# Deltanet attention and a top-2 router: expert sums kept in the output instead of rows gathered at the end

## The chip, the cores and the metric

The kernel runs on one core of a Trainium2 chip. The metric is the device time of one execution in microseconds. The inputs lie in device memory before it starts, and the output does after it.

## The reference

A gated delta-rule attention gives one row of 384 numbers for each of 3072 tokens; a noisy top-2 router then sends each token through two of eight experts, and the two results are added with weights.

```python
# attention: q, k, v are (4, 8, 768, 48), beta is (4, 8, 768)
k_n = k / (norm(k) + 1e-06)
for t in range(768):
    y[:, :, t] = einsum('bhd,bhde->bhe', q[:, :, t], state)
    v_old = einsum('bhde,bhd->bhe', state, k_n[:, :, t])
    state = state + beta_t * einsum('bhd,bhe->bhde', k_n[:, :, t], v[:, :, t] - v_old)
x = y.transpose(0, 2, 1, 3).reshape(3072, 384)
# router and experts: w1 is (8, 384, 1024), w2 is (8, 1024, 384)
noisy_logits = x @ w_gate + log1p(exp(x @ w_noise)) * noise
top2 = argpartition(-noisy_logits, 2)[:, :2]
top2_w = softmax over the two, with 1e-09 in the denominator
for e in range(8):
    for k in range(2):
        mask = top2[:, k] == e
        out[mask] += top2_w[mask, k, None] * (maximum(x[mask] @ w1[e], 0) @ w2[e])
```

## The kernel before

**Attention.** The 768 positions are cut into 12 chunks of 64, and two chunks are a step. A unit is one chunk of a pair of batches: 128 rows, 384 numbers each; a step has four units. `products(n)` transposes k of a unit (kp to kT) and makes its Gram matrices. `invert(s)` inverts the triangular matrices of a whole step on DVE by 30 pairs of operations that wait for each other (`part` and `t`, L340 and L344); its results are two transposes, `tt` (L355) and `tb` (L356). `join(n)` copies `tt` into `w64` on ACT (L369) and completes it with two products on TensorE (`p_x`), which go through ACT (`x`, L380, and `w64`, L389). `within(n)` transposes q (qp to qT, L269) and multiplies it with kT (`p_q`, then `qk` on DVE, L401). `recur(c)` is the serial part: `v` less what the state predicts (`p_b`, L472), `u`, then the new state `st`. `answer(n)` makes the output rows `y` (L427), and from them the router's logits. The loop over chunks takes a share of each of these at each point; a scheduler of the language then sets the order of every engine's instructions by its own estimates, so that a change in one place can move instructions in another.

**Router.** `route(s)` runs for each step: the two largest noisy logits, the weights, and for each token and choice a slot, which is the row of the expert's list that the token gets. `spread` then writes the token's rows to these slots of `rows_x` in device memory: eight scatters of 128 rows per step, issued by POOL. `rows_x` is cleared first, early in the program (eight SP DMAs), so that unused slots hold zeros.

**Experts.** Each expert has seven tiles of 128 rows, 896 in all. Its rows come in one DMA (`xr`), TensorE transposes them (`p_xt`, copied to `xe` by DVE), `first` multiplies with w1 and applies the relu on ACT (`hT`), and `second` multiplies with w2 (`p_o`) and has DVE copy the result out of PSUM to `yr` (L734), which SP writes to `rows_y`. The weights alternate between two pools; the second one is in memory that attention uses, so its first load waits until attention is over. All loads are issued by SP, in its order. Rows beyond 896 are handled in a branch (L768) that is taken only when some expert has more.

**The end.** For each of 24 tiles of 128 tokens POOL gathers the two expert rows of each token from `rows_y` (L795), ACT multiplies one by its weight (L802), DVE multiplies the other and adds (L803), and SP writes two pieces of the output (L810).

Of the kernel before, what the change touches and what calls it, by code (L numbers as in the profile page):

```python
# [15 lines left out]
C = 64  # L16
DP = 64
Q = 32
TILES = 7
HALF = TILES * 128 // 2  # L20


@with_exitstack
def kernel(
# [12 lines left out]
):  # L37

# [79 lines left out]
    rows_x = tc.dram_tile([E * N, DM], FP32, name="rows_x")  # L118
# [6 lines left out]
    slots = [const.tile([128, NT], I32, name=f"slot{i}") for i in range(2)]  # L125
    gates = [const.tile([128, NT], FP32, name=f"gate{i}") for i in range(2)]
# [35 lines left out]
    written, cleared = [], []  # L162

    def clear(buf, first, last):

        return nc.sync.dma_start(
            out=buf[first:last].rearrange("(t p) d -> p t d", p=128),
            in_=zero[:, None, :].to_broadcast([128, (last - first) // 128, DM]),
        ).ins
# [14 lines left out]
    def deltanet(ictx):  # L184
# [221 lines left out]
        def answer(n):  # L406
# [106 lines left out]
        def route(s):  # L513
# [20 lines left out]
            u, w, d, noisy = (full(x) for x in ("u", "w", "d", "noisy"))  # L534
            nc.scalar.activation(u, ln, ACTF.Abs)
# [19 lines left out]
            def take_largest(x, name):  # L555

                top, at, hit = (
                    per_token(f"{name}_top"), per_token(f"{name}_at"), full(f"{name}_hit")
                )
# [7 lines left out]
            top0, hit0 = take_largest(noisy, "a")  # L567
# [5 lines left out]
            top1, hit1 = take_largest(rest, "b")  # L573
            p1, den = gates[1][:, to], gates[0][:, to]
# [24 lines left out]
            for hit, slot in ((hit0, slots[0]), (hit1, slots[1])):  # L599
# [3 lines left out]
                nc.vector.tensor_copy(slot[:, to], row)  # L603
            for n in range(s * US, (s + 1) * US):
                for slot in slots:
                    yield
                    spread(ys[n], slot[:, n : n + 1])
# [4 lines left out]
            vv(p1, p1, den, ALU.mult)  # L612
# [21 lines left out]
        for e in range(E):  # L634
            cleared.append(clear(rows_x, e * N, e * N + TILES * 128))
        first_weights = load_weights(w_even, 0)

# [124 lines left out]
    most_i = moe.tile([128, 1], I32, name="most_i", bufs=1)  # L762
    p_n = ps([128, E], "p_n")
    nc.tensor.matmul(p_n, ones, before)
    nc.vector.tensor_reduce(out=most, in_=p_n, axis=AX.X, op=ALU.max)
    nc.vector.tensor_copy(most_i, most)
    count = nc.values_load(most_i[0:1, 0:1], min_val=0, max_val=N)
    with tc.If(count > TILES * 128):  # L768
        more = NT - TILES
        w1f = moe_w1.rearrange("e d f -> (e d) f")  # L770
        w2f = moe_w2.rearrange("e f d -> (e f) d")
        for e in range(E):
            with tc.tile_pool(name=f"left{e}", bufs=1) as pool:
# [3 lines left out]
                nc.sync.dma_start(out=w2e, in_=w2r[e])  # L777
                for i in range(TILES, NT):
                    r0 = e * N + i * 128
                    xr = pool.tile([128, 1, DM], FP32, name="xrl")  # L780
                    nc.sync.dma_start(out=xr[:, 0], in_=rows_x[r0 : r0 + 128])
                    xe = pool.tile([128, KT, 128], FP32, name="xel")
# [3 lines left out]
                    yr = pool.tile([128, DM], FP32, name="yrl")  # L786
                    second(w2e, hT, 0, yr)
                    nc.sync.dma_start(out=rows_y[r0 : r0 + 128], in_=yr)


    for n in range(NT):
        got = []
        for slot in slots:
            g = moe.tile([128, DM], FP32, name=f"got{len(got)}", bufs=4)
            nc.gpsimd.indirect_dma_start(  # L795
                out=g,
                out_offset=None,
                in_=rows_y,
                in_offset=bass.IndirectOffsetOnAxis(ap=slot[:, n : n + 1], axis=0),
            )  # L800
            got.append(g)
        nc.scalar.mul(got[0], got[0], gates[0][:, n : n + 1])  # L802
        nc.vector.scalar_tensor_tensor(  # L803
            out=got[0], in0=got[1], scalar=gates[1][:, n : n + 1], in1=got[0],
            op0=ALU.mult, op1=ALU.add,
        )
        c, u = divmod(n, NU)
        for i in range(2):
            t0 = (2 * u + i) * S + c * C
            nc.sync.dma_start(out=out[t0 : t0 + C, :], in_=got[0][i * C : i * C + C])  # L810
# [31 lines left out]
```

## Time and profile before

| | |
|---|---|
| time, median of 3 runs | 1200.49 us (1191.12 to 1205.19) |
| the profiled execution | 1196.75 us, its span 1195.0 us |
| mean granted TensorE clock | 0.813 |
| TensorE (PE) busy | 926.0 us, 77% |
| VectorE (DVE) busy | 325.7 us, 27% |
| ScalarE (ACT) busy | 272.5 us, 23% |
| GpSimd (POOL) busy | 170.7 us, 14% |
| moved by DMA | 124.30 MB, mean 104 GB/s |

The span is the time from the first to the last instruction that the profiler shows; the execution's own time is 1.75 us longer. The busy times are sums over the whole program, which has three stages with different limits: attention and router up to about 484 us, the experts from 511 to 1114 us, and the gathers at the end.

### The profile page before, as it was taken

To read this page: it belongs to the slowest core of one execution; us is meant where nothing else is said; L and a number is where in the kernel's file an instruction comes from. 1 tells how busy PE (TensorE), PEld (TensorE's weight loads), DVE (VectorE), ACT (ScalarE), POOL (GpSimd) and SP (SyncE) were. 2 spreads that over 40 slices of the span, in tenths; PEclk is the share of its full clock that TensorE was granted. 3 is DMA by queue.
4 is the path that set the end of the run, shared out by engine and by line. 5 is a ranking of instruction groups with operands and counts; after the bars stand their busy time and mean duration, and the time that the engine had idled before them with its cause. 6 is when DMAs were issued, how large, how long until landed. Compare 5 with 4: busy or idle time off the path is not lost. (4 is left out here: it accounts for less than half of the span.)

```text
span 1195.0 us, 20175 instructions
## 1 busy us (share of the span) xinstructions
PE 926.0 (77%) x8670; PEld 624.2 (52%) x8670; DVE 325.7 (27%) x875; ACT 272.5 (23%) x645; POOL 170.7 (14%) x222
## 2 busy tenths in 40 slices
PE   3265678788676788089999999999999999999200
PEld 2154667677565676055555555555555555555100
DVE  3867933736456130110200102001020010200122
ACT  3365254354241421011020110201102011020022
POOL 4211123141323111200000000000000000000365
PEclk9657566757666665589999999999999999999655
DMA  5981155234535701431302313023130220000366
GB/s 107 277 266 32 32 179 166 50 98 145 179 128 172 260 12 43 172 124 66 116 17 86 113 66 109 23 86 112 66 102 31 86 66 14 33 0 33 106 197 188
DMA packets 142657, 124.30 MB, mean 104 GB/s; under 512 B 84704, under 2 KB 134880, under 8 KB 142560
## 3 DMA queue, kind: packets, MB, share of 16 engines
q1 hardware_dynamic: 135520, 103.95, 27.9%
q0 software_dynamic: 6144, 18.88, 5.1%
q8 instruction: 70, 1.15, 0.4%
q14 instruction: 27, 0.22, 0.1%
q10 hardware_dynamic: 896, 0.10, 0.1%
HBM read 59.99 MB, written 62.91 MB: 103 GB/s over the span
## 5 line engine op out<-in xcount | busy, mean ns | idle before, releaser
L721 PE MATMUL p_h<-xe,w1e 128*128 128x448 f32 x768 | 291.0, 540 | 1.5 <-DVE xe L715 1.5
L730 PE MATMUL p_o<-w2e,hT 128*128 128x384 f32 x896 | 290.3, 486 | 0.0
L730 PEld LDWEIGHTS p_o<-w2e,hT 128*128 128x128 f32 x896 | 170.2, 190 | 119.6 <-issue 3.0
L721 PEld LDWEIGHTS p_h<-xe,w1e 128*128 128x128 f32 x768 | 145.5, 190 | 143.1 <-issue 139.9
L725 ACT ACTIVATE hT<-p_h 128x448 f32<-128x448 f32 x128 | 69.7, 544 | 527.8 <-PE p_h L721 527.8
L734 DVE COPY yr<-p_o 128x384 f32<-128x384 f32 x56 | 31.2, 557 | 543.4 <-PE p_o L730 543.4
L795 POOL DMA_INDIRECT got<-rows_y,slot x48 | 47.0, 979 | 644.4 <-SPq L768 625.5
L340 DVE TENSOR_TENSOR part<-t 128x30 f32<-128x30 f32 (+9 forms) x180 | 61.5, 342 | 4.8
L172 POOL DMA_INDIRECT rows_x<-y,slot x48 | 49.7, 1036 | 88.5 <-issue 41.8
L344 DVE TENSOR_TENSOR t<-t,part 128x30 f32<-128x30 f32 (+9 forms) x180 | 60.6, 337 | 4.7
L480 PE MATMUL p_u<-v,w 64*64 64x48 f32 x768 | 42.3, 281 | 9.3 <-ACT y L427 8.1
L510 POOL COPY wide<-st 64x384 f32<-64x384 f32 x44 | 23.5, 535 | 161.8 <-DVE st L507 145.7
L480 PEld LDWEIGHTS p_u<-v,w 64*64 64x64 f32 x768 | 40.0, 200 | 12.6 <-issue 9.7
L369 ACT COPY w<-tt 32x256 f32<-32x256 f32 x96 | 38.6, 402 | 31.2 <-DVE tt L355 29.8
L422 PE MATMUL p_y<-u,qk 64*64 64x48 f32 x768 | 45.0, 295 | 0.8 <-issue 0.8
L422 PEld LDWEIGHTS p_y<-u,qk 64*64 64x64 f32 x768 | 41.0, 209 | 5.2 <-issue 5.0
L714 PE MATMUL p_xt<-ident,xr 128*128 128x128 f32 x168 | 21.9, 291 | 27.9 <-DMA xr<-rows_x 27.9
L375 PE MATMUL p_x<-tb,at 32*32 32x32 f32 x768 | 23.4, 229 | 24.4 <-DVE tb L356 22.6
L277 PE MATMUL p_b<-st,kT 64*64 64x48 f32 x704 | 25.8, 269 | 18.9 <-DVE qk L401 15.1
L277 PE MATMUL p_k<-kT 64*64 64x64 f32 x768 | 21.4, 266 | 21.5 <-ACT kT L269 21.5
L802 ACT ACTIVATE got<-got,gate 128x384 f32<-128x384 f32 x24 | 14.7, 614 | 96.9 <-DMA got<-rows_y,slot 91.0
L277 PE MATMUL p_q<-qT,kT 64*64 64x64 f32 x768 | 17.6, 248 | 24.6 <-ACT qT L269 23.7
(121 smaller groups left out, 811.4 us busy)
## 6 DMA issues: line engine op xcount, KB each, us to landing
rows_y<-zero SPq DMA_DIRECT2D x8, 3264.0 KB
w1e<-in_moe_w_dram SPq DMA_DIRECT2D x8, 1536.0 KB
w2e<-in_moe_w_dram SPq DMA_DIRECT2D x8, 1536.0 KB
rows_x<-zero SPq DMA_DIRECT2D x8, 1344.0 KB
xr<-rows_x SPq DMA_DIRECT2D x8, 1344.0 KB
rows_y<-yr SPq DMA_DIRECT2D x56, 192.0 KB
kp<-in_k_dram SPq DMA_DIRECT2D x48, 96.0 KB
qp<-in_q_dram SPq DMA_DIRECT2D x48, 96.0 KB
```

The costliest lines, as they stand in the source:

```text
L172: d = nc.gpsimd.indirect_dma_start(out=rows_x, out_offset=bass.IndirectOffsetOnAxis(ap=slot, axis=0), in_=rows, in_offset=None,).ins
L277: nc.tensor.matmul(out[rows_of[b], z, j], lhsT[rows_of[z], j, rows_of[b]], rhs(rows_of[z], j, b), start=(j == 0), stop=(j == NP - 1), skip ...
L340: nc.vector.tensor_tensor(out=part, in0=t[:, j + 1 :, j, None].to_broadcast(shape), in1=t[:, None, j, 0:j].to_broadcast(shape), op=ALU.mult,)
L344: nc.vector.tensor_tensor(out=t[:, j + 1 :, 0:j], in0=t[:, j + 1 :, 0:j], in1=part, op=ALU.add)
L369: nc.scalar.copy(w64[rows, :, cols], tt[rows])
L422: nc.tensor.matmul(p_y[b, h], qk[b, h % 2, h // 2], u[b, h], start=(c == 0 and h == 0), stop=(h == H - 1), skip_group_check=True,)
L480: nc.tensor.matmul(p_u[b, h], w64[b, h], r[b, h], start=(h == 0), stop=(h == H - 1), skip_group_check=True,)
L721: nc.tensor.matmul(p_h, w1e[:, do, fo * 128 : (fo + 1) * 128], xe[:, do, cols], start=(do == 0), stop=(do == KT - 1),)
L725: nc.scalar.activation(hT[:, fo, cols], p_h, ACTF.Relu)
L730: nc.tensor.matmul(p_o, hT[:, fo, i * 128 : (i + 1) * 128], w2e[:, fo], start=(fo == 0), stop=(fo == FT - 1),)
L734: nc.vector.tensor_copy(yr, p_o)
L795: nc.gpsimd.indirect_dma_start(out=g, out_offset=None, in_=rows_y, in_offset=bass.IndirectOffsetOnAxis(ap=slot[:, n : n + 1], axis=0),)
```

## The change

A row of `rows_x` gets four numbers more: the token's number, the two weights and the first choice's expert. They are written beside the attention output, in a tile of four units (`ys[s]`, 388 numbers a row, with the number copied by POOL and the weights by DVE ahead of the scatters). The clear of `rows_x` writes 3072 as token number to unused slots, a number that gathers and scatters skip as out of bounds. `rows_y` and its clears are gone. The output itself is cleared early by one SP DMA of 128 x 24 x 384 numbers.

An expert now loads its `xr` ahead of the next expert's weights, takes index and weight of its rows from it on DVE, and gathers its tokens' sums so far from the output into `sums` (seven gathers on POOL; each waits for all seven scatters of the expert before). `second` multiplies PSUM by the weight and adds the sum (DVE), and a scatter writes each tile back to the output. The gathers, multiplications and writes behind the last expert are gone. The branch is changed in the same way.

```diff
+ROW = 384 + 4
-    rows_y = tc.dram_tile([E * N, DM], FP32, name="rows_y")
-    zero = const.tile([128, DM], FP32, name="zero")
-    nc.vector.memset(zero, 0.0)
+    empty = const.tile([128, ROW], FP32, name="empty")
+    nc.vector.memset(empty, 0.0)
+    nc.vector.memset(empty[:, DM : DM + 1], float(N))
...
-            y = sb([128, H, D], "y", 2 * US)
-            nc.scalar.copy(y, p_y)
-            yield
-            y_f = ys[n] = y.rearrange("p h d -> p (h d)")
+            if i == 0:
+                ys[s] = sb([128, US, ROW], "y", 2)
+            y_f = ys[s][:, i, 0:DM]
+            nc.scalar.copy(y_f, p_y.rearrange("p h d -> p (h d)"))
+            yield
...
+            num, gate1, gate0, expert0 = (ys[s][:, :, DM + x] for x in range(4))
+            nc.gpsimd.tensor_copy(
+                num, number.rearrange("p c u -> p (c u)")[:, s * US : (s + 1) * US]
+            )
...
+            vv(gate1, p1, den, ALU.mult)
+            vv(gate0, den, gate1, ALU.subtract)
+            for i in range(US):
                 for slot in slots:
                     yield
-                    spread(ys[n], slot[:, n : n + 1])
+                    spread(ys[s][:, i], slot[:, i : i + 1])
...
         first_weights = load_weights(w_even, 0)
+        added.append(
+            nc.sync.dma_start(
+                out=out.rearrange("(t p) d -> p t d", p=128),
+                in_=empty[:, None, 0:DM].to_broadcast([128, NT, DM]),
+            ).ins
+        )
...
-    def second(w2e, hT, i, yr):
+    def second(w2e, hT, i, gate, got):
...
-        nc.vector.tensor_copy(yr, p_o)
+        nc.vector.scalar_tensor_tensor(
+            out=got, in0=p_o, scalar=gate, in1=got, op0=ALU.mult, op1=ALU.add
+        )
+
+    def gates_of(xr, e, gate):
+
+        nc.vector.scalar_tensor_tensor(
+            out=gate, in0=xr[:, :, DM + 3], scalar=float(e - E), in1=xr[:, :, DM + 2],
+            op0=ALU.is_equal, op1=ALU.mult,
+        )
+        nc.vector.tensor_tensor(out=gate, in0=gate, in1=xr[:, :, DM + 1], op=ALU.add)
...
+    def gather(got, index, group, earlier):
+        return ordered(
+            nc.gpsimd.indirect_dma_start(
+                out=got, out_offset=None, in_=out,
+                in_offset=bass.IndirectOffsetOnAxis(ap=index, axis=0),
+                bounds_check=N - 1, oob_is_err=False,
+            ).ins, group, earlier,
+        )
...
     for e in range(E):
         w1e, w2e = weights
-        if e + 1 < E:
-            weights = load_weights(w_odd if e % 2 == 0 else w_even, e + 1)
         rows = slice(e * N, e * N + TILES * 128)
-        xr = moe.tile([128, TILES, DM], FP32, name="xr")
+        xr = moe.tile([128, TILES, ROW], FP32, name="xr")
...
-        clear(rows_y, e * N + TILES * 128, (e + 1) * N)
+        if e + 1 < E:
+            weights = load_weights(w_odd if e % 2 == 0 else w_even, e + 1)
+        index = moe.tile([128, TILES], I32, name="index")
+        nc.vector.tensor_copy(index, xr[:, :, DM])
+        gate = moe.tile([128, TILES], FP32, name="gate")
+        gates_of(xr, e, gate)
+        got = sums[e % 2]
+        gathers = [
+            gather(got[:, i], index[:, i : i + 1], f"out{e}", added) for i in range(TILES)
+        ]
+        added = []
...
         for i in range(TILES):
-            yr = moe.tile([128, DM], FP32, name="yr", bufs=3)
-            second(w2e, hT, i, yr)
-            r0 = e * N + i * 128
-            nc.sync.dma_start(out=rows_y[r0 : r0 + 128], in_=yr)
+            second(w2e, hT, i, gate[:, i : i + 1], got[:, i])
+            added.append(
+                scatter(got[:, i], index[:, i : i + 1], f"out{e}", gathers if i == 0 else [])
+            )
...
-    for n in range(NT):
-        got = []
-        for slot in slots:
-            g = moe.tile([128, DM], FP32, name=f"got{len(got)}", bufs=4)
-            nc.gpsimd.indirect_dma_start(
...
-        nc.scalar.mul(got[0], got[0], gates[0][:, n : n + 1])
...
-            nc.sync.dma_start(out=out[t0 : t0 + C, :], in_=got[0][i * C : i * C + C])
```

The order of instructions changes in places that the diff doesn't touch. The first is ACT in the second step of attention, while DVE works on the inverse of the step that follows it. Before, ACT has there (`tt` is that inverse, `x` and `w_` belong to join, `y`, `xT` and `logits` to answer, `kT` to products; a row's end says on which engine's signal it waits):

```order
L427 COPY y<-p_y 128x384 [waits PE_49]
L435 COPY xT<-p_xt 128x384 [waits PE_49]
L389 COPY w_1_151<-p_x 32x8x32 [waits PE_49]
L389 COPY w_1_151<-p_x 32x8x32
L447 COPY logits<-p_xt 128x16 [waits PE_49]
L427 COPY y<-p_y 128x384 [waits PE_49]
L369 COPY w_2_154<-tt 32x8x32 [waits DVE_49]
L369 COPY w_2_154<-tt 32x8x32 x3
L369 COPY w_3_157<-tt 32x8x32 x4
L269 COPY kT<-p_t 128x512 [waits PE_49]
```

After, the first copies from that same `tt` stand some twenty rows further ahead, between the two qT of the step (`root` is the first part of the inverse, L316 before and L320 now):

```order
L320 ACTIVATE root<-root 128x32 [waits Activation_49]
L273 COPY qT<-p_t 128x512 [waits PE_49]
L373 COPY w_2_153<-tt 32x8x32 [waits DVE_49]
L373 COPY w_2_153<-tt 32x8x32
L273 COPY qT<-p_t 128x512 [waits PE_49]
L384 ACTIVATE x<-p_x 32x256 [waits PE_49]
L384 ACTIVATE x<-p_x 32x256
L373 COPY w_2_153<-tt 32x8x32 x2
L373 COPY w_3_156<-tt 32x8x32 x3
L393 COPY w_4_159<-p_x 32x8x32 [waits PE_49]
```

Before, the two qT are neighbours and the copies from `tt` follow the second y; now everything that was between them stands behind the first two copies. On DVE the two `qk` and the two `v` of the step, which stood inside the inverse's chain, now stand behind its `tt`.

The second place is SP between attention and the experts. Before (`rows_y<-yr` are the first expert's results):

```order
L166 DMA rows_y<-zero 128x17x384 x2
L138 DMA w1e<-in_moe_w_dram 128x3x1024
L139 DMA w2e<-in_moe_w_dram 128x8x384
L742 DMA xr<-rows_x 128x7x384 x3
L138 DMA w1e<-in_moe_w_dram 128x3x1024
L758 DMA rows_y<-yr 128x384 x6
```

After:

```order
L798 DMA xr<-rows_x 128x7x388
L142 DMA w1e<-in_moe_w_dram 128x3x1024
L143 DMA w2e<-in_moe_w_dram 128x8x384
L798 DMA xr<-rows_x 128x7x388 x2
L142 DMA w1e<-in_moe_w_dram 128x3x1024
L143 DMA w2e<-in_moe_w_dram 128x8x384
L798 DMA xr<-rows_x 128x7x388
```

The rows of the first expert have moved ahead of the second expert's weights, and from the second expert on the SP queue holds loads only.

The third place is SP early in attention, behind the clears of `rows_x`. Before:

```order
L166 DMA rows_x<-zero 128x7x384 x8
L138 DMA w1e<-in_moe_w_dram 128x3x1024
L139 DMA w2e<-in_moe_w_dram 128x8x384
L257 DMA qp_140<-in_q_dram 64x8x48 x2
L257 DMA qp_142<-in_q_dram 64x8x48 x2
```

After:

```order
L170 DMA rows_x<-empty 128x7x388 x8
L142 DMA w1e<-in_moe_w_dram 128x3x1024
L143 DMA w2e<-in_moe_w_dram 128x8x384
L651 DMA out_dram<-empty 128x24x384
L261 DMA qp_139<-in_q_dram 64x8x48 x2
L261 DMA qp_141<-in_q_dram 64x8x48 x2
```

The output's clear stands between the first expert's weights and the second set of q and v loads.

## Rows read from the trace of the kernel before

**Rows 1.** The page's slices, 40 equal parts of the span, busy tenths of TensorE.

```profile
PE   3265678788676788089999999999999999999200
```

**Rows 2.** Windows: length, busy time (instructions) of each engine, granted clock, DMA share, GB/s.

```profile
520.00:600.00 80.00, 79.79 (x244) 44.41 (x243) 7.15 (x14) 9.80 (x18) 0.00 (x0) 1.00 0.23 81
...
1120.00:1195.00 75.00, 0.00 (x0) 0.00 (x0) 14.88 (x24) 14.75 (x24) 47.00 (x48) 0.50 0.67 189
```

**Rows 3.** Timeline where the experts end: start, busy time, engine, line, count, idle before.

```profile
1108.85 5.48 SPq L758 DMA_DIRECT2D rows_y<-yr  x2
...
1113.43 0.56 DVE L734 COPY yr<-p_o 128x384 f32<-128x384 f32 x1 [4.60 <-PE p_o L730]
...
1114.09 0.15 DVE L766 CAST most_i<-most 128x1 int32<-128x1 f32 x1
1120.39 0.98 POOL L795 DMA_INDIRECT got<-rows_y,slot  x1 [625.48 <-SPq L768]
```

**Rows 4.** Timeline of the last gathers and the end.

```profile
1185.07 1.22 POOL L795 DMA_INDIRECT got<-rows_y,slot  x1 [0.45 <-issue]
1185.50 5.75 SPq L810 DMA_DIRECT2D out_dram<-got  x8
...
1188.85 0.61 ACT L802 ACTIVATE got<-got,gate 128x384 f32<-128x384 f32 x1 [1.33 <-DMA got<-rows_y,slot]
1189.50 0.62 DVE L803 SCALAR_TENSOR_TENSOR got<-got,gate,got 128x384 f32<-128x384 f32 x1 [1.32 <-ACT got L802]
```

**Rows 5.** Timeline between attention and experts.

```profile
493.95 0.96 POOL L172 DMA_INDIRECT rows_x<-y,slot  x1 [0.30 <-issue]
496.90 0.37 SPq L138 DMA_DIRECT2D w1e<-in_moe_w_dram  x1
...
497.84 18.64 SPq L742 DMA_DIRECT2D xr<-rows_x  x3
...
511.37 4.72 PE L714 MATMUL p_xt<-ident,xr 128*128 128x128 f32 x21 [27.90 <-DMA xr<-rows_x]
```

**Rows 6.** Timeline of ACT around the second step's inverse.

```profile
117.24 0.59 ACT L269 COPY qT<-p_t 128x512 f32<-128x512 f32 x1 [2.27 <-PE p_t L267]
...
143.26 0.48 ACT L427 COPY y<-p_y 128x384 f32<-128x384 f32 x1 [3.19 <-PE p_y L422]
149.09 3.30 ACT L369 COPY w<-tt 32x256 f32<-32x256 f32 x8 [5.35 <-DVE tt L355]
152.41 0.59 ACT L269 COPY kT<-p_t 128x512 f32<-128x512 f32 x1
```

**Rows 7.** Timeline of DVE in the same stretch.

```profile
130.91 0.68 DVE L401 TENSOR_TENSOR qk<-p_q,mask 128x512 f32<-128x512 f32 x1
...
137.13 0.55 DVE L472 TENSOR_TENSOR v<-v,p_b 128x384 f32<-128x384 f32 x1
...
147.15 1.91 DVE L355 STREAM_TRANSPOSE tt<-scaled 128x1024 f32<-128x1024 f32 x1
```

**Rows 8.** Timeline of TensorE in the same stretch.

```profile
125.07 1.06 PE L375 MATMUL p_x<-tb,at 32*32 32x32 f32 x32
...
131.65 1.11 PE L277 MATMUL p_b<-st,kT 64*64 64x48 f32 x32 [5.13 <-DVE qk L401]
...
143.14 1.11 PE L267 MATMUL p_t<-ident,kp 128*128 128x128 f32 x4
...
153.05 1.13 PE L277 MATMUL p_k<-kT 64*64 64x64 f32 x32 [7.79 <-ACT kT L269]
```

**Rows 9.** Timeline, SP and TensorE: the second set of q loads and its first use.

```profile
65.37 13.63 SPq L257 DMA_DIRECT2D qp<-in_q_dram  x4
...
103.28 0.66 PE L267 MATMUL p_t<-ident,qp 128*128 128x128 f32 x4
```

**Rows 10.** Timeline of SP: the expert's rows, one issue per expert.

```profile
590.90 0.37 SPq L742 DMA_DIRECT2D xr<-rows_x  x1
...
665.87 0.37 SPq L742 DMA_DIRECT2D xr<-rows_x  x1
```

More of the change, by code (lines that the diff above doesn't have):

```diff
@@ L116 @@
     nc.vector.memset(ones, 1.0)
-    rows_x = tc.dram_tile([E * N, DM], FP32, name="rows_x")
-    rows_y = tc.dram_tile([E * N, DM], FP32, name="rows_y")
-    zero = const.tile([128, DM], FP32, name="zero")
-    nc.vector.memset(zero, 0.0)
-    slots = [const.tile([128, NT], I32, name=f"slot{i}") for i in range(2)]
-    gates = [const.tile([128, NT], FP32, name=f"gate{i}") for i in range(2)]
+    rows_x = tc.dram_tile([E * N, ROW], FP32, name="rows_x")
+    empty = const.tile([128, ROW], FP32, name="empty")
+    nc.vector.memset(empty, 0.0)
+    nc.vector.memset(empty[:, DM : DM + 1], float(N))
+    number = const.tile([128, NCH, NU], FP32, name="number")
+    for i in range(2):
+        nc.gpsimd.iota(
+            number[i * C : i * C + C], pattern=[[C, NCH], [2 * S, NU]], base=i * S,
+            channel_multiplier=1, allow_small_or_imprecise_dtypes=True,
+        )
     before = const.tile([128, E], FP32, name="before")
@@ L159, in load_router, with clear @@
         router["wgn"], router["noise"] = wgn, noise
-    written, cleared = [], []
-    def clear(buf, first, last):
+    written, cleared, added = [], [], []
+    def clear(e):
         return nc.sync.dma_start(
-            out=buf[first:last].rearrange("(t p) d -> p t d", p=128),
-            in_=zero[:, None, :].to_broadcast([128, (last - first) // 128, DM]),
+            out=rows_x[e * N : e * N + TILES * 128].rearrange("(t p) d -> p t d", p=128),
+            in_=empty[:, None, :].to_broadcast([128, TILES, ROW]),
         ).ins
@@ L602, in route @@
                 nc.vector.tensor_reduce(out=row, in_=mine, axis=AX.X, op=ALU.add)
[L603 to L607 removed]
+                slot = pool.tile(
+                    [128, US], I32, name=f"slot{len(slots)}", tag=f"slot{len(slots)}", bufs=2
+                )
+                nc.vector.tensor_copy(slot, row)
+                slots.append(slot)
             nc.vector.tensor_scalar(
@@ L733, in second, with ordered, scatter @@
             )
-        nc.vector.tensor_copy(yr, p_o)
+        nc.vector.scalar_tensor_tensor(
[7 more added lines that the diff above has]
+        nc.vector.tensor_tensor(out=gate, in0=gate, in1=xr[:, :, DM + 1], op=ALU.add)
+    def ordered(d, group, earlier):
+        tc.declare_no_dep(d, group=group, reason="no token has two rows of an expert")
+        tc.add_to_no_dep_group(group, d)
+        for i in earlier:
+            tc.add_manual_dep(d, i.name, SYNC, reason="sums so far of the same tokens")
+        return d
+    def gather(got, index, group, earlier):
[5 more added lines that the diff above has]
+            ).ins, group, earlier,
+        )
+    def scatter(got, index, group, earlier):
+        return ordered(
+            nc.gpsimd.indirect_dma_start(
+                out=out, out_offset=bass.IndirectOffsetOnAxis(ap=index, axis=0), in_=got,
+                in_offset=None, bounds_check=N - 1, oob_is_err=False,
+            ).ins, group, earlier,
+        )
+    sums = [moe.tile([128, TILES, DM], FP32, name=f"sums{i}", bufs=1) for i in range(2)]
+    for got in sums:
+        nc.gpsimd.memset(got, 0.0)
     for e in range(E):
         w1e, w2e = weights
-        if e + 1 < E:
-            weights = load_weights(w_odd if e % 2 == 0 else w_even, e + 1)
         rows = slice(e * N, e * N + TILES * 128)
-        xr = moe.tile([128, TILES, DM], FP32, name="xr")
+        xr = moe.tile([128, TILES, ROW], FP32, name="xr")
         d = nc.sync.dma_start(
@@ L777 @@
                 nc.sync.dma_start(out=w2e, in_=w2r[e])
+                earlier, added = added, []
                 for i in range(TILES, NT):
                     r0 = e * N + i * 128
-                    xr = pool.tile([128, 1, DM], FP32, name="xrl")
+                    xr = pool.tile([128, 1, ROW], FP32, name="xrl")
                     nc.sync.dma_start(out=xr[:, 0], in_=rows_x[r0 : r0 + 128])
+                    index = pool.tile([128, 1], I32, name="indexl")
+                    num, mine = (pool.tile([128, 1], FP32, name=x) for x in ("num", "mine"))
+                    nc.vector.tensor_copy(index, xr[:, :, DM])
+                    nc.vector.tensor_copy(num, index)
+                    nc.vector.tensor_tensor(
+                        out=mine, in0=place[:, i : i + 1], in1=counts[:, e : e + 1],
+                        op=ALU.is_lt,
+                    )
+                    nc.vector.tensor_scalar_sub(num, num, float(N))
+                    nc.vector.tensor_tensor(out=num, in0=num, in1=mine, op=ALU.mult)
+                    nc.vector.tensor_scalar_add(num, num, float(N))
+                    nc.vector.tensor_copy(index, num)
+                    gate = pool.tile([128, 1], FP32, name="gatel")
+                    gates_of(xr, e, gate)
+                    got = pool.tile([128, DM], FP32, name="gotl")
+                    nc.vector.memset(got, 0.0)
+                    mark = gather(got, index, f"left{e}", earlier)
                     xe = pool.tile([128, KT, 128], FP32, name="xel")
@@ L785 @@
                     first(w1e, xe, hT, slice(0, 128))
-                    yr = pool.tile([128, DM], FP32, name="yrl")
-                    second(w2e, hT, 0, yr)
-                    nc.sync.dma_start(out=rows_y[r0 : r0 + 128], in_=yr)
-    for n in range(NT):
-        got = []
-        for slot in slots:
-            g = moe.tile([128, DM], FP32, name=f"got{len(got)}", bufs=4)
-            nc.gpsimd.indirect_dma_start(
[L796 to L801, printed above, removed]
-        nc.scalar.mul(got[0], got[0], gates[0][:, n : n + 1])
[L803 to L809, printed above, removed]
-            nc.sync.dma_start(out=out[t0 : t0 + C, :], in_=got[0][i * C : i * C + C])
+                    second(w2e, hT, 0, gate, got)
+                    added.append(scatter(got, index, f"left{e}", [mark]))
 _INS = [
```

32 lines of the change are left out of this document (18 added, 14 removed).

## The prediction

> **What bounds the kernel now.** I read the page's slices first [rows 1]: TensorE is at 90% or more from the second half on and stands still in the last two slices, and in the first half it is never full. So there are three stages with three limits, and the busy share of 77% says little of any of them. The windows confirm it [rows 2]: inside the experts TensorE is busy 79.79 of 80 us at the full granted clock, while in the last 75 us it does nothing, POOL issues 48 gathers (47.00 us) and DVE and ACT work 15 us each.
>
> The timeline of the end gives the tail's shape. The last expert tile leaves PSUM at 1113.43, the count for the branch is cast at 1114.09, and the first gather starts only at 1120.39 [rows 3]. The 48th starts at 1185.07, its rows are used by ACT at 1188.85, DVE adds at 1189.50, the last output write is issued by 1191.25 and the span ends at 1195.0 [rows 4]. From 1113.43 to the end are 81.57 us, all of them on the path.
>
> Between attention and experts there is a second hole: the last scatter into the expert rows is issued at 493.95, SP issues two weight loads and then the expert's rows from 496.90, and TensorE starts at 511.37 after 27.90 us idle, released by the rows [rows 5]. In attention the engines wait for each other step by step; there the order on ACT, DVE and PE decides [rows 6 to 8].
>
> **The tail.** Removed: 48 gathers, 24 ACT multiplies, 24 DVE adds, 48 output writes. What stands there instead, from the last tile's start at 1113.43: a multiply-add on DVE, for which I take the 0.62 of the SBUF one in [rows 4] against 0.56 for the copy [rows 3]; one scatter on POOL, 0.96 to 1.22 and some 0.1 to get there [rows 4, 5], 1.1; its landing. Landing is bounded by 1.99 us (a scatter's end at 494.91 to the load that waited for it, 496.90 [rows 5]) and 2.56 (the last gather's end at 1186.29 to ACT [rows 4]); I take 2.56, since this scatter too ends alone on an idle queue. So the last write is in at 1117.7. The branch's load of the count waits for every outstanding DMA in both kernels: before, the last row write is issued by 1114.33 [rows 3], in by 1116.3 with the 1.99, and the first gather follows 4.1 us later. That is now at 1121.8. After the last landing the program needs 3.75 minus 1.99, about 1.8, to end: 1123.6. The tail shrinks from 81.6 to 10.2 us: **-71.4** (bounds -69 and -74, the second if the branch doesn't wait for the scatter).
>
> The Trainium skill ("DMA: Bandwidth & Descriptors", section "Anatomy of one DMA — SWDGE (gpsimd) path") gives 2.0 us plus the bytes at 436 GB/s for such a DMA; for 196,608 bytes that is an estimate of 2.45, and the sum would be 0.1 us less than with the 2.56 of this trace.
>
> **The expert's rows ahead of the weights.** In the before kernel 1.57 + 1.57 + 1.38 MB go out together at 496.90 and TensorE is released at 511.37: 14.47 us, of which 1.99 is latency, so 362 GB/s. The rows alone, now 1.39 MB, need 3.84 + 1.99, and are in at 502.7: **-8.5**. The lower bound is 0 (the weights are queued right behind and take their share of the same engines), the upper 12.5 (only the latency is left). I take 8.5, for the rows get their place in the queue before any byte of the weights. The weights of the second expert are needed only a period of 74.97 us later [rows 10]. The three small DVE operations on number and gate come ahead of the tiles' copies; each is like the 0.15 cast [rows 3], and they run while TensorE transposes the first tile: 0.
>
> The Trainium skill (same page, "Queues, rings and completion order") says that each engine consumes a ring's descriptors in ring order and that a completion signal lands after every earlier write of that engine: by it the rows wait for nothing behind them and the full 8.5 come, and no part of this trace shows them alone.
>
> **The moved instructions in attention.** This is the cost that the diff doesn't show. The order lists stand with the change: ACT now has the copy from the transposed inverse (tt) of the *next* step right behind the first qT, ahead of the second qT, of the x and of all that hangs on them. That inverse is the long DVE chain. Before, its tt starts at 147.15 and ACT copies it at 149.09 [rows 6, 7], long after the second qT (117.24) and the second y (143.26). Now ACT stands from 115 until tt is done. DVE in turn has the two qk (130.91 is the first) and the two v (137.13 the first) behind tt, no longer inside the chain; these four are 0.68 us and 0.55 us each [rows 7], 2.5 together, of which I take 1.7 for the chain, as neighbours on DVE overlap; so tt is done at 147.4 instead of 149.06. Then ACT does two copies (0.41 each, 3.30 for 8 [rows 6]) and the second qT at 148.2. From there the old chain runs again, link by link: from qT at 117.24 to the end of the last x product at 126.13 (125.07 + 1.06) 8.9 us [rows 6, 8], which puts that end at 157.1; the second p_b can follow at once, since the qk that it waited for until 131.65 is now early; from p_b to the end of the kp transposes at 144.25 are 12.6 us [rows 8], so kT starts on ACT at 169.7. Before it started at 152.41 [rows 6], and TensorE waited for it. **+17**. Bounds: +8, if the x and y work has slack that I don't see (the six other copies on ACT, 2.5 us, were counted as filling gaps), and +20, if they don't fit in gaps. It isn't made up later: the next steps are the same serial chain, and their order is as it was.
>
> **The output cleared early.** One SP DMA of 4.72 MB goes between the first weights and the second set of q loads. At 362 GB/s it takes 13 us in a queue that is full then. Before, the four q loads are issued from 65.37 to 79.00 and so in by about 81; now by 94, and TensorE transposes them at 103.28 [rows 9]. v is needed later still. I take +1 for instructions that arrive late beside it, with bounds of 0 and 6.
>
> **At nothing, with the cover named.** The eight rows_y clears go: 0 to -2, since they run beside attention, whose engines wait for each other and not for transfers. Rows of 388 instead of 384 numbers add 1% to scatters and clears. The gates move ahead of the scatters on DVE; one 0.15 operation more is on the path in the last step. Together -1.
>
> The new chain between experts is hidden: last multiply-add 0.62, scatter 1.1, landing 2.56, seven gathers at 1.26 (0.96 + 0.30 [rows 5]), landing 2.56: 15.7 us. The next expert's first multiply-add comes a period minus six tiles later, 74.97 - 6 x 5.16 = 44.0 (5.16 is the 4.60 idle and 0.56 busy [rows 3, 10]). 28 us are to spare at each of seven borders; if they were gone, each us over would cost seven. Behind the waiting gathers on POOL stand only the scatters of the same expert.
>
> **The sum.** 1195.0 - 71.4 - 8.5 + 17 + 1 - 1 = 1132.1 us of span, 1133.9 with the 1.75 around it. The profiled execution took 1196.75 and the median of the runs shown is 1200.49; I add that difference and forecast **1137**.
>
> **Rivals.** (1) *The moved ACT copy costs little*, because its wait is met sooner or the chain has slack: 1137 - 17 = 1120. For it speaks that attention's engines are never full [rows 1]; against it, that TensorE stands 7.79 us for the very kT that is delayed [rows 8]. (2) *The rows gain nothing* because weights and rows share the engines: 1145. Against it, the order of issue. (3) *The early clear delays attention*: TensorE and ACT wait 5 to 8 us more: 1143. It decides if the q loads come over 9 us later than I have them. (4) *The border between experts shows a little*, or gathers and scatters slow the weight loads: 1 to 4 us for each of seven, 1145 to 1165. (5) *Slower than before*: the gathers wait behind the scatters' landing in turn. It begins when one gather costs more than (44.0 - 6.9) / 7 = 5.3 us, and at 7.2 us each border loses 13 us, 93 together: 1230. A gather that waits for the landing of the one before would be 0.96 + 2.56 = 3.5, still hidden. (6) *The tail stays long*, the branch's end and the drain costing tens of us that the gathers covered before: 1150 to 1180; nothing in the rows shows such work.
>
> **How the numbers follow.** The forecast has 0.60 (1128 to 1148 by its bounds), rival 1 0.19 (1114 to 1125), rival 2 0.05, rival 3 0.06, rival 4 0.05, rival 5 0.03, rival 6 0.02. The range 1115 to 1149 takes in the forecast, nearly all of rival 1, and 2 and 3. The three runs of before lie between 1191 and 1205, so about 1% is what can be told from no change. Faster by more than that: all but rival 5 and a part of 4 and 6, 0.95; within 0.02; slower 0.03.
>
> **What would show it.** TensorE's second p_q of the second step starts near 149 instead of 118, and kT near 170; if kT is near 152 to 155, rival 1 holds. Behind the last scatter into the expert rows, the 14.5 us from SP's first issue to the first transposes become 6; if it is over 12, rival 2. The expert period stays within 0.3 us of 74.97; if the first multiply-add waits for a gather, rival 4 or 5. From the last tile's multiply-add to the end 10 us; over 13 and the tail's sum is wrong. The second qp transposes of the first steps wait for no DMA, or else rival 3.

## The result, and the profile after

| | before | changed |
|---|---|---|
| median | 1199.72 us (4 runs, 1191.12 to 1205.19) | 1133.37 us (4 runs, 1131.0 to 1135.87) |
| ratio, 95% interval | | 0.9453 [0.9393, 0.9514] |
| profiled execution, span | 1195.0 us | 1131.1 us |
| mean granted clock | 0.813 | 0.825 |

The changed kernel is 66 us faster, 3.6 us below the 1137 on record. A second pair, in another set of runs, gave 0.9421 [0.935, 0.9493]; there the kernel before took 1179 us. All ratios are of fast runs alone, which leaves two of four for the clear beside the experts below (0.9231; the median of all four gives 0.932).

The page of the changed kernel: its span, and the busy tenths and the granted clock in 40 slices.

```profile
span 1131.1 us, 20168 instructions
...
PE   2258147877958688827999999999999999999995
...
PEclk9655558675666656558999999999999999999998
```

The two empty slices at the end [rows 1] are gone. Where the time went is read at fixed points of the two profiles:

| point | before | changed | difference |
|---|---|---|---|
| first qT of the second step [rows 6 give the second] | 114.38 | 121.29 | +6.9 |
| kT of the third step [rows 6] | 152.41 | 173.47 | +21.1 |
| last scatter into the expert rows [rows 5] | 493.95 | 505.27 | +11.3 |
| TensorE's first transpose of an expert [rows 5] | 511.37 | 514.76 | +3.4 |
| last tile out of PSUM [rows 3] | 1113.43 | 1117.18 | +3.8 |
| end | 1195.0 | 1131.1 | -63.9 |

ACT around the second step's inverse (start, busy, line, count, idle before), the first qT of the kernel before and then the changed kernel:

```profile
114.38 0.59 ACT L269 COPY qT<-p_t 128x512 f32<-128x512 f32 x1
```

```profile
121.29 0.58 ACT L273 COPY qT<-p_t 128x512 f32<-128x512 f32 x1
154.31 0.82 ACT L373 COPY w<-tt 32x256 f32<-32x256 f32 x2 [32.43 <-DVE tt L359]
155.15 0.58 ACT L273 COPY qT<-p_t 128x512 f32<-128x512 f32 x1
...
172.89 0.48 ACT L433 COPY y<-p_y 128x384 f32<-128x384 f32 x1 [1.71 <-PE p_y L426]
173.47 0.59 ACT L273 COPY kT<-p_t 128x512 f32<-128x512 f32 x1
```

DVE and TensorE in the same stretch:

```profile
152.37 1.90 DVE L359 STREAM_TRANSPOSE tt<-scaled 128x1024 f32<-128x1024 f32 x1
154.14 0.66 DVE L405 TENSOR_TENSOR qk<-p_q,mask 128x512 f32<-128x512 f32 x1
```

```profile
155.79 1.13 PE L281 MATMUL p_q<-qT,kT 64*64 64x64 f32 x32 [30.69 <-ACT qT L273]
...
172.77 0.66 PE L271 MATMUL p_t<-ident,kp 128*128 128x128 f32 x4
```

ACT stands 32.43 us until tt is done at 154.27, and only then makes the second qT, which was at 117.24 [rows 6]; TensorE stands 30.69 us for it. That is the moved copy as forecast.

Between attention and experts, behind the last scatter into the expert rows, the rows now go first; TensorE starts 6.3 us behind SP's first issue, where it was 14.5 [rows 5]:

```profile
505.27 0.96 POOL L176 DMA_INDIRECT rows_x<-y,slot  x1 [0.30 <-issue]
...
508.42 0.38 SPq L798 DMA_DIRECT2D xr<-rows_x  x1
508.85 0.56 SPq L142 DMA_DIRECT2D w1e<-in_moe_w_dram  x1
...
514.76 4.71 PE L733 MATMUL p_xt<-ident,xr 128*128 128x128 f32 x21 [19.98 <-DMA xr<-rows_x]
```

The experts' period is read from two issues of SP, 75.03 us against 74.97 [rows 10], and DVE's sums waited for TensorE alone in all 56 cases, never for a gather:

```profile
594.23 0.37 SPq L798 DMA_DIRECT2D xr<-rows_x  x1
...
669.26 0.37 SPq L798 DMA_DIRECT2D xr<-rows_x  x1
```

```profile
DVE sums L754 <- PE p_o L750: 508.4, 56, 40.2
```

The end: the last sum and the last scatter. From 1117.18 to 1131.1 are 13.9 us; the 48 gathers and all behind them [rows 3, 4] were 81.6.

```profile
1117.18 0.62 DVE L754 SCALAR_TENSOR_TENSOR sums<-p_o,gate,sums 128x384 f32<-128x384 f32 x1 [4.54 <-PE p_o L750]
...
1118.07 0.98 POOL L785 DMA_INDIRECT out_dram<-sums,index  x1 [4.18 <-DVE most L838]
```

### The profile page after: what moved, and what is told of

Its sections match the earlier page's. It is cut to its first block, busy times and chain, and to the rows that moved or that the text cites. A ratio compares the mean times of both kernels' runs of the same rounds, so it can differ in the third digit from the quotient of the medians.

```text
span 1131.1 us, 20168 instructions
## 1 busy us (share of the span) xinstructions
PE 933.2 (83%) x8670; PEld 631.0 (56%) x8670; DVE 314.1 (28%) x883; ACT 257.4 (23%) x621; POOL 239.8 (21%) x297
## 4 chain that ended last, share of the span: by engine, by line
PE 70%; DVE 11%; issue 6%; ACT 6%; another core or an unknown queue 2%; DMA 1%; POOL 1%; ACTq 1%; SPq 0%; DVEq 0%; POOLq 0%
PE p_h L740 26%; PE p_o L750 26%; PE p_y L426 3%; DVE t L348 2%; DVE part L344 2%; PE p_y L420 2%; PE p_u L485 2%; PE p_xt L446 2%; PE p_x L388 2%; ACT w L373 2%; ACT gd L304 1%; PE p_x L379 1%; PE p_xt L438 1%; PE p_b L281 1%
## 5 line engine op out<-in xcount | busy, mean ns | idle before, releaser
L754 DVE SCALAR_TENSOR_TENSOR sums<-p_o,gate,sums 128x384 f32<-128x384 f32 x56 | 34.6, 617 | 508.4 <-PE p_o L750 508.4
L785 POOL DMA_INDIRECT out_dram<-sums,index x56 | 55.6, 993 | 438.6 <-DVE sums L754 428.8
L776 POOL DMA_INDIRECT sums<-out_dram,index x56 | 56.5, 1010 | 55.2 <-issue 38.5
L485 PEld LDWEIGHTS p_u<-v,w 64*64 64x64 f32 x768 | 40.6, 202 | 13.8 <-ACT y L433 6.8
L281 PEld LDWEIGHTS p_q<-qT,kT 64*64 64x64 f32 x768 | 16.4, 164 | 54.7 <-ACT qT L273 52.3
L459 POOL TENSOR_TENSOR v<-v,norms 128x384 f32<-128x384 f32 x24 | 21.1, 892 | 99.3 <-DMA v<-in_v_dram 84.4
```

The source lines that it names most:

```text
L281: nc.tensor.matmul(out[rows_of[b], z, j], lhsT[rows_of[z], j, rows_of[b]], rhs(rows_of[z], j, b), start=(j == 0), stop=(j == NP - 1), skip ...
L485: nc.tensor.matmul(p_u[b, h], w64[b, h], r[b, h], start=(h == 0), stop=(h == H - 1), skip_group_check=True,)
L776: nc.gpsimd.indirect_dma_start(out=got, out_offset=None, in_=out, in_offset=bass.IndirectOffsetOnAxis(ap=index, axis=0), bounds_check=N - ...
L785: nc.gpsimd.indirect_dma_start(out=out, out_offset=bass.IndirectOffsetOnAxis(ap=index, axis=0), in_=got, in_offset=None, bounds_check=N - ...
```

## The experiments

The experiments went in three sets of runs, each on one chip. The ratios are to the kernel before in the same set, which took 1171, 1179 and 1175 us in the three.

**The rows_y clears moved.** In the kernel before:

```diff
-        clear(rows_y, e * N + TILES * 128, (e + 1) * N)
+        z = clear(rows_y, e * N + TILES * 128, (e + 1) * N)
+        tc.add_manual_dep(z, d.name, SYNC, reason="clear beside the experts")
```

> The kernel before, with each of the eight rows_y clears held until the expert's rows have landed, so that none runs beside attention. Theory 'fetch': a clear of 3.3 MB beside attention makes TensorE wait for its next instructions (2.87, 1.90 and 2.60 us gaps at 341, 407 and 414 us of the kernel before) and keeps its clock at the lower level; then attention ends about 9 us earlier and the time is near 1191. Theory 'slack' (the changed kernel made up 10 of its 21 us late in attention because the chain has room there, and the clears cost nothing, as the prediction had it, 0 to 2): near 1199. Both: the experts' period stays at 75.0.

Measured: 0.9965 [0.9919, 1.0012] over ten runs. TensorE's gaps for want of an instruction are gone from the profile from the third step on, but the time moves by 4 us with an interval of -9.5 to +1.4. The 9 us of the theory are at its edge, the prediction's 0 to 2 inside.

**The clear of the output in three other places.** The lines that issue it are taken out behind the first weights and put behind the first expert's loads (from where the scheduler draws them into the middle of attention); the same with a dependence on the expert's rows; and behind the q loads of the second set:

```diff
         first_weights = load_weights(w_even, 0)
-        added.append(nc.sync.dma_start(out=out..., in_=empty...).ins)
...
         for n in range(NU):
             now(within(n))
+        added.append(nc.sync.dma_start(out=out..., in_=empty...).ins)   # clear behind q
...
+        if e == 0:
+            z = nc.sync.dma_start(out=out..., in_=empty...).ins
+            tc.add_manual_dep(z, d.name, SYNC, ...)   # beside the experts alone
+            added.append(z)
```

> The changed kernel with the output's clear written behind the first expert's loads in the program; the scheduler puts it in the middle of attention, where the first rows_y clear was, and ACT, DVE and POOL keep the order that they had in the kernel before. Theory 'order and fetch': the 14 us of the moved ACT copies and the 7 us of the early clear are gone, and the clear costs up to 3 us where it is now: 1112 to 1116. Theory 'slack': only the 11.5 us by which attention ended later come back at most: 1122. Theory 'late loads' (all 21 us came from q and v that arrived late, none from the order): as 'order and fetch', 1112 to 1116, so the next-but-one run tells these two apart.

> As the run before, with the clear held until the first expert's rows have landed, so that nothing large runs beside attention. 'Order and fetch': 1133 - 21 = 1112, kT of the third step at 152.5 as before, the last scatter into the expert rows 20 us earlier than in the changed kernel, at 484. 'Slack': 1122, the last scatter at 494. In both the first expert's gathers wait for the clear until about 525, and its first sum is due at 550, so nothing is lost there.

> The changed kernel with the early clear written two loads later, behind the q loads of the second set. The engines' order is that of the kernel before, and the clear still runs early, from some 75 to 93 us. Theory 'order': the 14 us come back and the 7 of the early clear stay, 1119, with TensorE's granted clock at the lower level between 90 and 103 us. Theory 'late loads': q is in time now and v isn't; if the loads were the cause, up to 21 come back, 1112, with the clock high between 90 and 103. Theory 'the order costs nothing': 1133 less what q gives.

Measured: 0.9279 [0.9191, 0.9367] in mid attention, 0.9231 [0.9135, 0.9327] beside the experts, 0.9293 [0.9216, 0.937] behind q, against 0.9453 and 0.9421 for the changed kernel. On the scale of the first pair these are 1113, 1107 and 1115 us, nearer to 'order and fetch' than to 'slack'; but the intervals of the first and the third take in both theories, and the second, run again below, comes to 1118 (0.932). So the times show that something comes back, and the traces have to say what. All three have ACT's old order. With the clear beside the experts kT of the third step is back where it was:

```profile
153.05 0.59 ACT L273 COPY kT<-p_t 128x512 f32<-128x512 f32 x1
```

The run behind q separates order and clear. Its ACT:

```profile
116.38 0.58 ACT L273 COPY qT<-p_t 128x512 f32<-128x512 f32 x1
119.23 0.58 ACT L273 COPY qT<-p_t 128x512 f32<-128x512 f32 x1 [2.27 <-PE p_t L271]
...
150.38 3.30 ACT L373 COPY w<-tt 32x256 f32<-32x256 f32 x8 [8.27 <-DVE tt L359]
153.70 0.58 ACT L273 COPY kT<-p_t 128x512 f32<-128x512 f32 x1
```

From the first qT to kT are 37.3 us, as in the kernel before (38.0) and not as in the changed one (52.2); the 4.7 MB still go beside attention early. So with ACT's old order, and the two qk of DVE in their old place, kT is back at 153.70. Not every engine has its old order here, against what I expected of this run: on POOL and DVE the two v of the step still stand behind the inverse, as in the changed kernel, and kT doesn't feel it:

```profile
151.99 0.98 DVE L477 TENSOR_TENSOR v<-v,p_b 128x384 f32<-128x384 f32 x2
```

'Late loads' falls by the traces, for in the changed kernel TensorE's second set of qp transposes (112.42) waits for no load either, and 'order' holds; the time alone, 1115, lies between the two (1112 and 1119). What is left of the early clear is in the windows (busy time with instructions, granted clock, DMA share, GB/s), here of the kernel before, the changed one and the one behind q:

```profile
80.00:90.00 10.00, 9.02 (x222) 7.80 (x222) 5.23 (x14) 4.77 (x12) 2.09 (x4) 0.68 0.43 80
90.00:103.00 13.00, 11.19 (x366) 10.09 (x363) 12.07 (x34) 6.91 (x18) 0.47 (x2) 1.00 0.25 49
```

```profile
80.00:90.00 10.00, 7.89 (x199) 6.87 (x199) 4.91 (x12) 4.57 (x11) 2.39 (x4) 0.67 1.06 396
90.00:103.00 13.00, 12.40 (x196) 10.91 (x198) 10.62 (x27) 2.78 (x6) 0.20 (x2) 0.50 0.61 140
```

```profile
80.00:90.00 10.00, 8.19 (x267) 7.14 (x264) 8.46 (x20) 4.31 (x11) 2.65 (x5) 0.80 0.95 294
90.00:103.00 13.00, 9.63 (x147) 8.46 (x146) 10.88 (x31) 3.76 (x10) 0.16 (x1) 0.61 0.85 235
```

With the DMA engines full between 80 and 90 us the changed kernel's TensorE waits for an instruction while no engine is awaited, and the granted clock is then at its lower level (0.50 of 2.4 GHz) to 103, where it was at the upper one in the kernel before:

```profile
90.03 0.37 PE L281 MATMUL p_q<-qT,kT 64*64 64x64 f32 x1 [1.28 <-issue]
```

In the eight profiles without the early clear the granted clock between 90 and 103 us was 0.87 to 1.00 and the first qT stood at 111.2 to 115.1; in the six with it the clock was 0.50 to 0.74 in five and 1.00 in one, and qT at 115.7 to 121.3. The means, 113.1 and 117.8, put the early clear at 4.7 us. The one with the clock at 1.00 (the run without the branch, below) had its qT at 115.7 all the same, so the clock can't be the whole of it.

**Both kernels again, on one chip with the next two.**

> The kernel before, unchanged, for a profile on the same chip as the three kernels beside it. If the eight clears of rows_y hold attention up (theory 'fetch'), its TensorE shows gaps of 2 to 3 us before p_x or p_b while no engine is awaited, each within 15 us of a clear's issue, and attention ends 5 to 20 us later than in the kernels without them (last scatter into the expert rows near 494 against 472 to 474). If not, it ends near 474 too, and the difference of the two first profiles was the chip's or the run's.

> The changed kernel, unchanged, on this chip: 0.945 of the kernel before. The late kT of the third step near 173 us, the last scatter into the expert rows 15 to 20 us behind that of a kernel whose order and clear are as before, the expert's rows at TensorE 6.3 us behind their issue, the end 13 to 14 us behind the last tile.

Measured: 0.9421 for the changed kernel. The first qT of the second step, kT of the third and the last scatter, in the kernel before and in the changed one:

```profile
111.44 0.59 ACT L269 COPY qT<-p_t 128x512 f32<-128x512 f32 x1
...
149.47 0.59 ACT L269 COPY kT<-p_t 128x512 f32<-128x512 f32 x1
...
473.97 0.96 POOL L172 DMA_INDIRECT rows_x<-y,slot  x1 [0.30 <-issue]
```

```profile
117.25 0.59 ACT L273 COPY qT<-p_t 128x512 f32<-128x512 f32 x1
...
170.59 0.59 ACT L273 COPY kT<-p_t 128x512 f32<-128x512 f32 x1 [0.37 <-PE p_t L271]
...
473.05 0.96 POOL L176 DMA_INDIRECT rows_x<-y,slot  x1 [0.30 <-issue]
```

The kernel before had its last scatter at 473.97, not 494, so the 20 us between its first profile and the runs above were the chip's or the run's, and not the price of the rows_y clears. TensorE's gaps add up to 7.2 us from the third step on. The changed kernel's kT is 21.1 us behind, as in the first pair, and its last scatter not behind at all, against my expectation of 15 to 20.

**Five times the gathers.** 28 gathers more per expert, into tiles that nothing reads:

```diff
+        for k in range(28):
+            extra.append(ordered(nc.gpsimd.indirect_dma_start(out=sink[:, k % 14],
+                in_=out, in_offset=IndirectOffsetOnAxis(ap=index[:, k % TILES : k % TILES + 1], axis=0),
+                ...).ins, f"out{e}", added + ...))
         gathers = [
```

> The changed kernel with 28 more gathers per expert ahead of the seven, into tiles that nothing reads; every one waits for the scatters of the expert before like the seven. The prediction's chain between experts then takes 6.9 + 35 x 1.26 = 51 us against the 44 us to the next expert's first sum: 7 us lost at each of seven borders, 50 to 60 in all, and TensorE idle for want of PSUM. Rival (the chain isn't hidden today, the gathers' landing or their traffic already costs): more than 28 x 1.26 = 35 us per border, 250 in all. Rival (POOL's pace doesn't matter, the gathers run ahead): no change.

Measured: 1104.5 us in one run, beside 1107.15 for the changed kernel (1099.4 to 1115.79); nothing lost that these can show. POOL's first gather that counts starts at 607.41 (POOL, then DVE, then TensorE):

```profile
607.41 1.00 POOL L776 DMA_INDIRECT sums<-out_dram,index  x1 [0.30 <-issue]
```

```profile
611.09 0.62 DVE L754 SCALAR_TENSOR_TENSOR sums<-p_o,gate,sums 128x384 f32<-128x384 f32 x1 [40.49 <-DMA sums<-out_dram,index]
612.54 0.62 DVE L754 SCALAR_TENSOR_TENSOR sums<-p_o,gate,sums 128x384 f32<-128x384 f32 x1 [0.83 <-PE p_o L750]
```

```profile
602.02 36.28 PE L750 MATMUL p_o<-w2e,hT 128*128 128x384 f32 x112
638.14 2.46 PE L733 MATMUL p_xt<-ident,xr 128*128 128x128 f32 x21
```

The first sum is 3.7 us late (611.09; the changed kernel has 5.4 us from an expert's first p_o to its first sum, which puts it at 607.4), the second is in time again, and TensorE goes from p_o to the next expert without a gap. In six of the experts the first sum waits for its gather like this, and TensorE never waits for a sum. The prediction's chain had the sum of a tile wait for all seven gathers; it waits only for its own, and PSUM holds the tile that DVE can't take yet. The cover is wider than the 28 us of the prediction.

**The count made and loaded ahead of the experts**, with the clear beside the experts:

```diff
+    (counts, most, most_i, p_n and count = nc.values_load(...) moved here)
     sums = [moe.tile([128, TILES, DM], FP32, name=f"sums{i}", bufs=1) for i in range(2)]
```

> The output's clear beside the experts as in the run of that name, and the count for the branch made and loaded from ahead of the experts, so that the branch behind them needn't wait for it or for the last scatter's landing. The changed kernel's tail is 13.9 us from the last tile's multiply-add, the prediction had 10.2. If the load of the count behind the landing is what the sum missed, the tail falls to 9 to 10 and the time to 4 us below the clear beside the experts; if the rest is the branch itself and the end of the program, it stays at 13 to 14.

Measured: 0.9242 [0.9159, 0.9325]. The tail:

```profile
span 1089.6 us, 20168 instructions
```

```profile
1076.89 0.62 DVE L748 SCALAR_TENSOR_TENSOR sums<-p_o,gate,sums 128x384 f32<-128x384 f32 x1 [4.54 <-PE p_o L744]
```

12.7 us, where the other profiles of the new end with the branch have 12.8 to 14.3: the wait for count and landing is some 1.5 us of it at most, so the first of the two expectations falls. The last scatter into the expert rows was at 465.14 here, with the old order in attention, and so 7.9 us ahead of the changed kernel's in the same set; the medians of four are 1093.89 and 1107.15 us.

**The clears put back** beside attention, into a buffer that nothing reads, and their base once more:

```diff
+        nc.sync.dma_start(out=rows_z[e * N + TILES * 128 : (e + 1) * N]..., in_=empty...)
```

> The kernel with the clear beside the experts, and beside attention eight clears of 3.3 MB into a buffer that nothing reads, at the places in SP's order where the rows_y clears stood in the kernel before. Theory 'fetch': TensorE's gaps with no engine awaited come back, 7 to 10 us in all from the third step on (10.5 and 7.2 in the two profiles of the kernel before, 0 without the clears), and the time rises by 4 to 10 us over the kernel beside it. Prediction's 'at nothing': 0 to 2.

> The kernel with the clear beside the experts, once more as the base for the run with the clears put back and as the fastest version so far: 0.923 of the kernel before.

Measured: 0.9342 [0.9302, 0.9382] with the clears, 0.932 [0.928, 0.9359] without. TensorE's waits for an instruction (us in total, times, longest) with and without:

```profile
PE p_x L389 <- issue: 4.3, 2, 2.2
...
PE p_b L282 <- issue: 2.8, 2, 2.5
```

```profile
PE p_y L426 <- issue: 1.1, 1, 1.1
```

The gaps come back, 7.1 us from the third step on, and the time hardly follows: 2.6 us, and the intervals overlap. 'Fetch' is right on the gaps; that they cost 4 to 10 us isn't shown.

**The rows behind the weights again.**

```diff
+        if e + 1 < E:
+            weights = load_weights(w_odd if e % 2 == 0 else w_even, e + 1)
         xr = moe.tile([128, TILES, ROW], FP32, name="xr")
...
-        if e + 1 < E:
-            weights = load_weights(w_odd if e % 2 == 0 else w_even, e + 1)
```

> The changed kernel with the expert's rows loaded behind the next expert's weights, as in the kernel before. From SP's first issue between attention and experts to TensorE's first transpose 14.5 us again instead of 6.3, so 8 us of the span; the output's clear, the order in attention and the tail as in the changed kernel. If the rows' place in the queue were not the cause, it stays at 6.

Measured: 1116.93 us in one run, 0.951 of the kernel before in that set, and in the timeline 14.5 us from 484.17 to 498.65:

```profile
484.17 0.38 SPq L142 DMA_DIRECT2D w1e<-in_moe_w_dram  x1
...
485.12 18.64 SPq L800 DMA_DIRECT2D xr<-rows_x  x3
...
498.65 4.71 PE L733 MATMUL p_xt<-ident,xr 128*128 128x128 f32 x21 [28.14 <-DMA xr<-rows_x]
```

**No branch.** All from the load of the count to the end of the branch is taken out.

> The changed kernel without the branch for more than 896 rows of an expert, and without the load of the count; what it leaves out is the handling of such rows. The tail from the last multiply-add was 13.9 us, with 1.9 to the end of the last scatter's issue. If load and branch stand in the way of the end, it falls by 4 to 6, to 8 to 10; if the rest is the last scatter's landing and the end of any program, it stays within 2.

Measured: 1109.29 us in one run; from the last sum at 1100.20 to the end 7.2 us, 6.7 less than the 13.9:

```profile
span 1107.4 us, 20088 instructions
```

```profile
1100.20 0.62 DVE L754 SCALAR_TENSOR_TENSOR sums<-p_o,gate,sums 128x384 f32<-128x384 f32 x1 [4.54 <-PE p_o L750]
```

## Why the prediction was right, point by point

The place and the sign hold. That the sum is met within 1 us of span (1131.1 against 1132.1) is partly luck: attention came out 5.7 us less late than forecast (+11.3 at the last scatter against +17), and the tail 3.7 us too long.

- **The tail**, -71.4 forecast with bounds of -69 and -74, -67.7 measured in the first pair (81.6 to 13.9) and -63.9 in the second (77.7 to 13.8). By the prediction's own sign (over 13 us left) its sum was wrong. The step that was too small is the branch: the sum has 4.1 us from the last landing to what follows it, and the run without the branch ends 6.7 us sooner behind its last sum, 5.5 to 7.1 against all profiles with the branch. What in the branch costs this isn't shown; that its load of the count waits for the landing, as the prediction had it, is some 1.5 us at most. The rest, 7.2 us from the last sum, is near the 6.1 that the sum's other terms give (0.62 + 1.1 + 2.56 + 1.8).
- **The rows ahead of the weights**, -8.5 forecast, -8.1 measured, and 14.5 us again with the order undone. Rival 2 is out. By the Trainium skill ("DMA: Bandwidth & Descriptors", "Queues, rings and completion order") each engine takes a ring's descriptors in ring order, from which the prediction had the rows wait for nothing behind them; these traces agree, 6.3 against 14.5.
- **The moved instructions**, +17 forecast. From the first qT to kT are 52.18 us instead of 38.03, +14.2, and in the second pair 53.3 instead of 38.0, +15.3. The links were right (tt at 154.27 is 5.2 later, that is 1.7 earlier against the shift of the early clear, as summed); the chain from tt to kT took 19.2 us instead of the 22.3 summed, because TensorE's last links ran at a higher clock than before (granted 0.98 from 168 to 174 us, where the same links had 0.50 before; p_t takes 0.66 us for 4 at 172.77 and took 1.11 [rows 8]). Rival 1 is out: with the old order kT is at 153.
- **The early clear**, +1 forecast with 0 to 6 as bounds, +6.9 in the first pair, +5.8 in the second and 4.7 over all profiles: mis-sized. The loads were in time, as forecast; by the windows it cost TensorE's gap and the lower clock behind it, of which the sum had one us for "instructions that arrive late" and nothing for the clock. That the gap holds the clock down isn't shown. So rival 3's price of 5 to 8 was about met, though not by its condition, late q loads.
- **At nothing**, -1: the clears' removal is worth 4.1 and 2.6 us by the two comparisons made for it, neither clear of zero. The chain between experts is hidden, with more cover than was counted (rivals 4 and 5 out).
- **"It isn't made up later"** is the sentence of the prediction that failed. The third step's first new state comes 20 us late in both pairs (181.62 against 161.60, 178.74 against 159.26), the last scatter 11.3 us late in the first pair and not late in the second. In the first pair TensorE's waits for an instruction in between fall from 10.5 to 1.2 us, about what is made up (8.7), though the clears put back brought 7.1 us of such waits and hardly any time. In the second they fall from 7.2 to 0.8, and TensorE's work takes 22 us less at a higher granted clock (0.64 before, 0.71 changed; the columns as in the windows above):

```profile
159.00:474.00 315.00, 245.54 (x4920) 218.06 (x4913) 146.84 (x475) 114.84 (x305) 89.27 (x105) 0.64 0.44 138
```

```profile
179.00:473.00 294.00, 223.51 (x4888) 198.45 (x4888) 145.64 (x479) 113.87 (x303) 88.25 (x108) 0.71 0.22 58
```

- **Open:** what sets that clock. It was 0.66 to 0.71 in the four later profiles with the late kT and 0.62 to 0.66 in the others of those chips. The loss was not all made up: beside kernels with the old order on the same chip the last scatter came 8 and 11 us later in two profiles with the late kT (473.05 and 476.30 against 465.14) and 10 to 18 in two others (481.01 and 488.25 against 470.31 and 471.46). By the times, the old order and a clear elsewhere are worth 1.0 to 2.2% (0.9231 to 0.932 against 0.9453 and 0.9421), 12 to 26 us.

The fastest versions have the old order on ACT: 0.9231 and 0.932 with the output's clear beside the experts, 0.9279 in mid attention, 0.9293 behind q. Their intervals overlap, so which place is best isn't shown.

## What to carry to other kernels

Read how a change moves the other engines' instructions before costing it: here one transfer put early changed ACT's order, and that put a step of attention back by 14 to 15 us with no load late. Where such a transfer stands in the program can be changed without changing what it does, so try two or three places and compare the orders. A delay in a serial stage can come back in part behind it, so read it at the stage's end too. Work at the end of a program that only rearranges results can often be done in the shadow of the stage that makes them.

## What was not expected of the hardware

- While the DMA engines were full (share 0.95 to 1.06), TensorE stood 1.1 to 3.6 us in all for instructions that no engine held up (0 to 1.1 without the transfer), and in five of six profiles its mean granted clock in the next 13 us was 0.50 to 0.74, where it was 0.87 to 1.00 without the transfer.
- A branch that isn't taken, with the load of its count, cost 5.5 to 7.1 us at the end of the program (one profile without it against ten with it).
- The same kernel took 1171 to 1200 us in the medians of four sets of runs, a wider spread than most of the effects here, so only ratios within a set could be used.
